# A decode step on one core: eight of its 131 loads get a second DMA with eight outer groups

## The chip, the cores and the metric

One NeuronCore of a Trainium2 chip runs the whole program. The time is device microseconds (us) of one execution. Beside the times of plain runs there is one profiled execution with its trace: instructions of each engine (PE is the matrix engine TensorE with its weight loads PEld, DVE is VectorE, ACT ScalarE, POOL GpSimd, SP SyncE, which here only issues DMAs), the packets of the DMA queues, and the increments of semaphores. The core has 16 DMA engines.

## What is computed

One token goes through a pre-norm attention block with a cache and then a small dense block:

```python
q = (layernorm(x) @ wq).reshape(1, 1, 32, 128).transpose(0, 2, 1, 3)
scores = einsum("bhqd,bhkd->bhqk", q, k_cache) * 128 ** -0.5   # 32 heads, 32768 keys
p = softmax(scores)
o = einsum("bhqk,bhkd->bhqd", p, v_cache)
h = x + o.transpose(0, 2, 1, 3).reshape(1, 1, 4096) @ wo
t = einsum("bsd,df->bsf", layernorm(h), w1) + b1               # 512 -> 1376
out = h + einsum("bsf,fd->bsd", t * tanh(softplus(t)), w2)
```

All data is bf16. The two caches are 256 MB each (MB of 2^20 bytes), the weights some 11 MB. Each byte of the caches is read once and used for one query only. The sum over keys doesn't depend on their order, so long as the K row and the V row of a key stand at the same place.

## The kernel before

**Loads and slots.** The caches are read in halves of a head: 16384 rows of 128 numbers, 4 MB, laid on 128 partitions as 128 rows each, 32 KB a partition in one run. The list `order` (lines 186 to 193) has 131 loads: `wq`; K of head 0 in two halves; then, for t from 0 to 30, K half 0 of head t+1, V half 0 of head t, K half 1 of head t+1, V half 1 of head t; then `wo`, `w12` (w1 and w2, three DMAs) and the two halves of V of head 31. So load 3 is K(1,0), 11 is K(3,0), 16 is V(3,0), 126 is V(30,1), 127 is wo, 128 is w12, 129 and 130 are V(31,0) and V(31,1).

The ring in SBUF has `NS = 6` slots of 4 MB; load i goes to slot i % 6. All loads are issued by SP, in this order (lines 231 to 255). Before load i SP waits until PE has used load i-6 up (line 234, `free_name`), and it issues nothing past such a wait. The last load is cut into four pieces of 64, 32, 16 and 16 rows a partition with semaphores of their own (`TAIL`, lines 195 and 248 to 253).

**Readiness.** A DMA adds 16 to the semaphore of its slot, one for each engine's share. A slot's loads share one semaphore, so `ready_wait` (lines 201 to 203) gives PE the count that stands for "this load and all before it in this slot": 16 times the number of DMAs issued to the slot so far, with two more after w12.

**Work on a half of K** (`k_group`, lines 321 to 346): 16 groups of 8 blocks of 128 rows. PE transposes the 8 blocks into PSUM (line 340), DVE copies the 128 x 1024 result to SBUF (line 343), and two groups later PE multiplies each transposed block with q (line 313, `scores`), which gives one column of 128 scores a block. **Work on a half of V** (`pv`, line 365): 128 matmuls that add up the 128 x 1 output, weighted with the probabilities. Between them stands the softmax of a head (lines 377 to 397): maximum over columns (DVE, 378), over partitions (PE 382, DVE 384), broadcast (PE 387, DVE 389), exponential (ACT 390), sum (PE 395, DVE 397).

**Order on PE** (lines 412 to 422): for each t the first K half of head t+1, the first V half of head t, the second K half, the second V half with the steps of the softmax in between. At the end (lines 435 to 475) come the projections with wo of heads 0 to 30 (431), the softmax sum and b1 (395, 439), V of head 31 (365), its projection (431), the second layer norm (280 to 290), w1 (457), the activation (461 to 467), w2 (472) and the sum (475), whose result SP writes out (256).

**Code.** PE's part alone is 25118 matmuls and as many weight loads. [...]

## Time and profile before

| | |
|---|---|
| median of 3 runs | 1329.84 us (1328.77 to 1330.07) |
| profiled execution: its own time | 1330.19 us |
| profiled execution: span, first to last instruction | 1328.4 us |
| PE busy | 1106.9 us (83%), 25118 matmuls |
| PE weight loads busy | 1073.6 us (81%) |
| DVE busy | 721.7 us (54%) |
| ACT, POOL busy | 20.6 and 1.7 us |
| granted TensorE clock, mean | 0.755 |
| DMA | 551.40 MB in 24080 packets, 415 GB/s over the span |
| PE transposes, line 340 | 8192, 755.7 us, 248 ns each |
| DVE copies, line 343 | 1024, 681.7 us, 692 ns each |
| PE scores, line 313 | 8192, 368.0 us, 166 ns each |
| PE with V, line 365 | 8192, 236.7 us, 164 ns each |
| a 4 MB load of K, issue to landing | 39.6 us, median of 64 |
| a 4 MB load of V, issue to landing | 43.5 us, median of 63 |

Busy times of lines overlap, since PE pipelines its matmuls. In a row of the timeline stand the start in us, the time in us, engine, line, operation, result and sources, how many instructions the row merges, and in brackets the idle time of the engine before it with what ended it; "issue" there means that the profile shows nothing that the engine waited for. The packet is a DMA engine's unit: a partition's run of 32 KB is one packet.

### The profile page before, as it was taken

How to read it: one execution, taken by the hardware profiler on the slowest of the kernel's cores; microseconds unless marked ns; L12 is line 12 of the kernel's file. 1: busy time of each engine (PE TensorE's matmuls, PEld its weight loads, DVE VectorE, ACT ScalarE, POOL GpSimd, SP SyncE). 2: the span in 40 equal slices, each digit the busy share in tenths (PEclk: the TensorE clock that was granted, in tenths of full speed). 3: DMA queues.
4: the chain of work that ended last, by engine and by line, in shares of the span. 5: the costliest groups of instructions: out<-in, count | busy, mean ns of one | idle time of the engine just before them, and what ended most of it. 6: DMA issues, size and time to landing. Idle time of an engine off the chain costs nothing.

```text
span 1328.4 us, 51752 instructions
## 1 busy us (share of the span) xinstructions
PE 1106.9 (83%) x25118; PEld 1073.6 (81%) x25118; DVE 721.7 (54%) x1210; ACT 20.6 (2%) x70; POOL 1.7 (0%) x8
## 2 busy tenths in 40 slices
PE   3887888988888988889889888888888988887984
PEld 3887887888887988888878888788887988887884
DVE  2754655655655654646556556556556555645540
ACT  0000000000000000000000000000000000000000
POOL 0000000000000000000000000000000000000000
PEclk9877868777878777667778667777778677768775
DMA  9999999999999999999999999999999999999974
GB/s 389 429 429 426 432 426 425 433 426 428 431 424 432 427 426 432 425 425 434 426 428 429 425 425 422 424 427 417 428 425 428 425 427 425 426 411 431 383 281 195
DMA packets 24080, 551.40 MB, mean 415 GB/s; under 512 B 2528, under 2 KB 6720, under 8 KB 6976
## 3 DMA queue, kind: packets, MB, share of 16 engines
q1 hardware_dynamic: 23664, 548.09, 96.9%
q8 instruction: 196, 3.21, 1.0%
q14 instruction: 12, 0.10, 0.0%
q10 hardware_dynamic: 144, 0.00, 0.0%
q0 software_dynamic: 64, 0.00, 0.0%
HBM read 548.08 MB, written 0.00 MB: 413 GB/s over the span
## 4 chain that ended last, share of the span: by engine, by line
PE 75%; issue 13%; DVE 8%; DMA 4%; SPq 0%; ACT 0%
PE tps L340 43%; PE ops L365 16%; PE sps L313 12%; DVE ering L343 7%; DMA ring<-in_A_v_cache_dram 2%; DMA ring<-in_A_k_cache_dram 2%; PE hlp L387 1%; PE hlp L382 1%; PE hlp L395 1%; PE sps L457 0%; SPq L229 0%; PE sps L472 0%; PE hlp L282 0%; DVE pmax L378 0%; ACT lns L287 0%
## 5 line engine op out<-in xcount | busy, mean ns | idle before, releaser
L343 DVE COPY ering<-tps 128x1024 bf16<-128x1024 bf16 x1024 | 681.7, 692 | 368.9 <-PE tps L340 365.9
L340 PE MATMUL tps<-identb,ring 128*128 128x128 bf16 x8192 | 755.7, 248 | 35.4 <-issue 31.7
L340 PEld LDWEIGHTS tps<-identb,ring 128*128 128x128 bf16 x8192 | 583.2, 112 | 42.6 <-issue 38.7
L313 PE MATMUL sps<-qT,ering 128*128 128x1 bf16 x8192 | 368.0, 166 | 39.9 <-issue 30.3
L313 PEld LDWEIGHTS sps<-qT,ering 128*128 128x128 bf16 x8192 | 340.4, 101 | 46.8 <-issue 33.5
L365 PE MATMUL ops<-pbuf,ring 128*128 128x1 bf16 x8192 | 236.7, 164 | 114.9 <-issue 106.3
L365 PEld LDWEIGHTS ops<-pbuf,ring 128*128 128x128 bf16 x8192 | 224.7, 101 | 131.6 <-issue 122.7
L373 DVE TENSOR_TENSOR oT<-ops,rtotc 128x1 bf16<-128x1 f32 x32 | 5.1, 161 | 93.5 <-PE ops L365 93.5
L384 DVE TENSOR_REDUCE gmax<-hlp 1x1 f32<-1x128 f32 x32 | 8.9, 279 | 77.2 <-PE hlp L382 77.2
L390 ACT ACTIVATE pbuf<-sps,nbias 128x256 bf16<-128x256 f32 x32 | 15.2, 474 | 1256.5 <-DVE nbias L389 1256.5
L378 DVE TENSOR_REDUCE pmax<-sps 128x1 f32<-128x256 f32 x32 | 13.6, 425 | 17.0 <-PE sps L313 17.0
L387 PE MATMUL hlp<-gmax,onesmat 1*128 1x1 f32 x64 | 18.7, 356 | 2.7 <-issue 2.3
L387 PEld LDWEIGHTS hlp<-gmax,onesmat 1*128 1x128 f32 x64 | 15.8, 303 | 3.7 <-issue 2.4
L382 PE MATMUL hlp<-ident,pmax 128*1 128x128 f32 x64 | 16.9, 357 | 1.7 <-issue 1.2
L282 PE MATMUL hlp<-lns,meanmat 128*128 128x2 f32 x4 | 1.2, 364 | 16.4 <-DVE lns L281 16.4
L282 PEld LDWEIGHTS hlp<-lns,meanmat 128*128 128x128 f32 x4 | 1.0, 313 | 16.5 <-DVE lns L281 16.5
L395 PE MATMUL hlp<-esum,onesmat 128*128 128x1 f32 x64 | 14.2, 292 | 0.0
L389 DVE TENSOR_SCALAR nbias<-hlp 128x1 f32<-128x1 f32 x32 | 5.1, 158 | 13.9 <-PE hlp L387 13.9
L395 PEld LDWEIGHTS hlp<-esum,onesmat 128*128 128x128 f32 x64 | 12.2, 239 | 0.0
L397 DVE RECIPROCAL rtotc<-hlp 128x1 f32<-128x1 f32 x32 | 5.2, 162 | 6.3 <-PE hlp L395 6.3
L274 DVE CAST lnx<-xb 128x4 f32<-128x4 bf16 x1 | 0.2, 171 | 13.6 <-DMA xb<-in_A_x_dram 13.6
L431 PE MATMUL yps<-oT,ring 128*128 128x1 bf16 x128 | 4.7, 172 | 1.9 <-issue 1.6
(43 smaller groups left out, 39.4 us busy)
## 6 DMA issues: line engine op xcount, KB each, us to landing
ring<-in_A_k_cache_dram SPq DMA_DIRECT2D x64, 4096.0 KB, 39.6
ring<-in_A_v_cache_dram SPq DMA_DIRECT2D x63, 4096.0 KB, 43.5
ring<-in_A_wq_dram SPq DMA_DIRECT2D x1, 4096.0 KB, 14.2
ring<-in_A_wo_dram SPq DMA_DIRECT2D x1, 4096.0 KB, 43.5
ring<-in_A_v_cache_dram SPq DMA_DIRECT2D x1, 2048.0 KB, 26.0
ring<-in_B_w_dram SPq DMA_DIRECT2D x1, 1376.0 KB, 39.1
ring<-in_B_w_dram SPq DMA_DIRECT2D x1, 1280.0 KB, 9.2
ring<-in_A_v_cache_dram SPq DMA_DIRECT2D x1, 1024.0 KB, 28.9
```

The costliest lines, as they stand in the source:

```text
L313: S.step(PE, lambda r=r: t_.matmul(S_b[h % 2][:, col0 + r:col0 + r + 1], ering[:, bg % NE, r, :], qT[:, h:h + 1], start=True, stop=True), ...
L340: S.step(PE, lambda r=r: t_.matmul(tb[:, r * 128:(r + 1) * 128], kt[:, gi * GT + r, :], identb[:, :], is_transpose=True, start=True, stop= ...
L343: S.step(DVE, lambda: v.tensor_copy(ering[:, bg % NE, :, :].rearrange("p r d -> p (r d)"), tb[:, :]), name=f"ev{bg}", waits=[f"trb{bg}"] + ...
L365: S.step(PE, lambda r=r, col=col: t_.matmul(o_ps[:, h % 2:h % 2 + 1], vt[:, r, :], pbuf[:, h % 2, col:col + 1], start=(col == 0), stop=(co ...
L373: S.step(DVE, lambda: v.tensor_tensor(oT[:, h:h + 1], o_ps[:, h % 2:h % 2 + 1], rtotc[:, h:h + 1], ALU.mult), name=f"oev{h}", waits=[f"pv{ ...
L378: S.step(DVE, lambda: v.tensor_reduce(pmax[:, h:h + 1], S_b[h % 2][:, 0:SCOLS], AXX, ALU.max), name=f"pmax{h}", waits=[f"qkh{h}"])
L382: S.step(PE, lambda: t_.matmul(A_REG, pmax[:, h:h + 1], ident[:, :], start=True, stop=True), name=f"A{h}", waits=[f"pmax{h}", "ident"])
L384: S.step(DVE, lambda: v.tensor_reduce(gmax[0:1, h:h + 1], A_REG, AXX, ALU.max), name=f"gmax{h}", waits=[f"A{h}"])
L387: S.step(PE, lambda: t_.matmul(B_REG, onesm[0:1, :], gmax[0:1, h:h + 1], start=True, stop=True), name=f"B{h}", waits=[f"gmax{h}", "consts0"])
L390: S.step(ACT, lambda: a.activation(pbuf[:, h % 2, :], S_b[h % 2][:, 0:SCOLS], ACTF.Exp, bias=nb[:, h:h + 1], scale=SC, accum_out=esum[:, h ...
L395: S.step(PE, lambda: t_.matmul(C_REG, onesm[:, :], esum[:, h:h + 1], start=True, stop=True), name=f"C{h}", waits=[f"exp{h}"])
L397: S.step(DVE, lambda: v.reciprocal(rtotc[:, h:h + 1], C_REG), name=f"rcp{h}", waits=[f"C{h}"])
```

## The change

In eight loads, K and V half 0 of heads 3, 11, 19 and 27 (places 11, 16, 43, 48, 75, 80, 107 and 112 of the order), the 4 MB come in two DMAs. The first brings 96 rows a partition (3 MB): partition p gets rows 96p to 96p+95 of the half. The second brings the other 32 rows a partition (1 MB) from the last 4096 rows of the half. Its source pattern has an outer dimension of 8, then 16, then a run of 32 rows: block 8b+a of 32 rows goes to partition 16a+b. Its target is 128 partitions with 8 KB each, as it was. So the rows of a half stand in another order than before, the same one for K and for V. `ready_wait` counts the DMAs of the slot from a table of how many each load has, and gives the same counts as before where no shifted load stands in the slot.

```diff
+    SHIFTED = {(h, 0) for h in range(3, H, 8)}
+    MAIN = 96
+    EXTRA = TPS - MAIN
+
+    def shifted(what):
+        return what[0] in ("k", "v") and what[1:] in SHIFTED
+
+    def dmas(what):
+        return 3 if what[0] == "w12" else 2 if shifted(what) else 1
+
     def ready_wait(what):
         i = where[what]
-        return (ready[i % NS], 16 * (i // NS + 1 + (2 if i % NS == where[("w12",)] % NS and i >= where[("w12",)] else 0)))
+        return (ready[i % NS], 16 * sum(dmas(order[n]) for n in range(i % NS, i + 1, NS)))
...
                     assert at == TPS
+                elif shifted(what):
+                    both = cache[0, h, half * 128 * TPS:(half + 1) * 128 * TPS, :]
+                    start(flat[:, 0:MAIN * Dh], both[0:128 * MAIN, :].rearrange("(p r) d -> p (r d)", r=MAIN), ready[slot])
+                    start(flat[:, MAIN * Dh:], both[128 * MAIN:, :].rearrange("(b a r) d -> a b (r d)", a=8, b=16), ready[slot])
                 else:
                     start(flat, rows, ready[slot])
```

## The prediction

> **What bounds the kernel now.** I read the page first (slices, queues), then the waits, SP's own rows, the tail's timeline, and last the 16 completion increments of each load, which the trace keeps one by one.

> The page's slices and queues:

> ```profile
> DMA  9999999999999999999999999999999999999974
> ...
> q1 hardware_dynamic: 23664, 548.09, 96.9%
> q8 instruction: 196, 3.21, 1.0%
> ```

> The DMA engines never rest before the last two slices. Beside the data (q1) a second queue, q8, fetches PE's code: 196 packets of 16 KB.

> The waits, whole span (engine, line, releaser: total us, times, longest):

> ```profile
> PE ops L365 <- issue: 106.3, 59, 3.2
> ...
> PE ops L365 <- DMA ring<-in_A_v_cache_dram: 8.5, 5, 5.6
> ...
> PE tps L340 <- DMA ring<-in_A_k_cache_dram: 3.3, 1, 3.3
> ```

> PE waits for data six times in all: for the first load, and for the last two. In between it is paced by itself (its work, gaps named "issue", VectorE's copies). Per load the trace agrees: between loads 3 and 126 each K or V has landed 2.5 to 14.6 us before PE's first use of it. Four loads take PE (1250.36-53.33)/30 = 39.9 us (first uses of loads 3 and 123) and the DMA engines, as below, 40.0, so both look full, but the margin is the DMA's.

> The increments show what the mean share hides. Time (us) of the 1st, 8th, 9th and 16th of one load's increments, loads of one ring slot (extracted from the trace):

> ```
> load  issue     1st      8th      9th     16th
>   0    0.74    13.25    13.57    13.79    14.94
>  30  272.74   304.53   307.33   312.35   315.54
>  54  509.03   537.55   542.28   553.07   554.76
>  78  751.09   770.69   777.29   792.78   795.56
> 126 1230.49  1246.01  1248.09  1272.99  1275.83
> ```

> The engines are two groups of eight. The eight ahead need (770.69-13.25)/78 = 9.71 us a load, which is eight 32 KB packets of 1.214 us (median of 16384). The eight behind need (795.56-14.94)/78 = 10.008 us: 0.298 more. That is the code: the q8 packets' durations repeat with period eight (1018, 1018, 1073, 1069, 1060, 1100, 1099, 1087 ns), one per engine in turn, one per engine every 53 us or 5.4 loads, 1.6 us lost each. From load 79 on the eight ahead have nothing queued: their part of a load lands some 12 us after its issue. One of them, the 8th, also lags by 5 us in 78 loads.

> The lag is paid at the end. SP's rows, then PE's:

> ```profile
> 1243.36 0.38 SPq L229 DMA_DIRECT2D ring<-in_A_wo_dram  x1
> 1249.95 32.32 SPq L229 DMA_DIRECT2D ring<-in_B_w_dram  x3
> 1282.32 2.52 SPq L229 DMA_DIRECT2D ring<-in_A_v_cache_dram  x5
> ```

> ```profile
> 1297.91 0.60 PE L439 MATMUL sps<-b1f,ident 128*128 128x11 f32 x2 [0.33 <-DVE b1f L438]
> 1304.07 3.57 PE L365 MATMUL ops<-pbuf,ring 128*128 128x1 bf16 x128 [5.56 <-DMA ring<-in_A_v_cache_dram]
> ...
> 1310.51 1.04 PE L365 MATMUL ops<-pbuf,ring 128*128 128x1 bf16 x33 [0.56 <-issue]
> ...
> 1314.75 0.59 PE L365 MATMUL ops<-pbuf,ring 128*128 128x1 bf16 x16 [0.66 <-DMA ring<-in_A_v_cache_dram]
> ```

> SP hangs in w12's issue from 1249.95: the first of the three lasts 31.1 us, to 1281.05, which is 5.2 us after the engines behind are through load 126 and into wo (4096 packets of 1 KB). The last V loads go out at 1282, though their slots were free at 1265.41 and 1270.67 (PE's last use of loads 123 and 124). PE is ready for them at 1298.51, waits to 1304.07, then follows the pieces to 1315.34; 13.0 us of work follow that nothing shortens.

> **The change, part by part.** The profiled execution took 1330.19 us with a span of 1328.4; the median of the runs is 1329.84, so what I work out against 1330.19 lies 0.3 us above it.

> Issues: 8 more of 0.33 us on SP, which waits 872 + 345 us for free slots; nothing. PE, VectorE and ScalarE run the same instructions; the permuted rows are the same in K and V. The wait of a shifted load now counts 32 increments of its slot: queued behind it on PE is the whole stream, and it costs only if the later DMA lands after PE's first use.

> Transfers: the main DMA moves 24 KB per partition, so 8 packets of 3/4 x 1.214 = 0.911 us per engine, 7.28 us for 9.71: every engine saves 2.43. The second moves 128 pieces of 8 KB. I take it that eight outer groups mean eight engines with 16 pieces each; 8 KB packets exist in before (the tail's 32-row piece: median 0.312 us), so 16 x 0.312 = 4.99 us. New is that an engine's pieces lie 64 KB apart in the cache; the nearest scattered row is wo, 1 KB pieces at 46 ns, so 0.368 us for 8 KB: at most 16 x 0.056 x 8 = 7.2 us more on those eight, and 1 us less at the 24 KB rate. I take 0.312, the same size. Eight engines gain 2.57 us of work a load, eight lose 2.43. Over 8 loads: +20.5 and -19.4 us.

> Which eight? No row of before names an engine, and every load there uses all sixteen. That is the unknown, and it has two ends: the group ahead (forecast), or one with an engine from behind in it (rival A).

> [...]

> If the work goes to the group ahead: the group behind is through load 126 at 1275.83 - 19.4 = 1256.4. The group ahead, never short of work now, at 13.57 + 126 x 9.71 + 20.5 = 1257.5, its laggard some 8 us later (5 us in 78 loads), 1265.6. SP comes free 5.2 us after the last of these, at about 1271, and the last V loads go out at once: 11 us earlier. On that laggard wo (11 us, as the group behind takes from 1275.83 to 1286.86), w12 (7.3, to 1294.12), V 31,0 (9.9) and V 31,1 (10.7) follow one another: the last piece lands at 1304.5 for 1314.7 (1311.7 with the dear 8 KB pieces).

> What is late next is PE itself. At 1298.51 it starts the 256 matmuls with V: 3.57 us for the first 128 (as measured), 4.0 for the rest (the 128 in the rows from 1308.97 sum to 0.99+1.04+1.01+0.59+0.59 = 4.2, 31 to 37 ns each), so 1306.1 without gaps: 9.2 us earlier. But code arrives in blocks of 128 matmuls, and the wait that goes covered its fetch: in before one gap (1310.51, 0.56) was left of two. Uncovered gaps in these phases are 1.6 us (1293.88, project) to 2.7 (mid-run, the chain's longest "issue" pieces). Two of 2.7 leave 3.8 us of gain; I take two of 1.5, near the two nearest rows (0.97 at 1287.67, 1.61 at 1293.89): 1309.1, so 6.2 us. The middle gains nothing, since PE doesn't wait there. Forecast: 1330.2 - 6.2 = **1324.0**, own range 1320 to 1327.

> **Rivals.**

> A, slower: the eight engines of the second DMA are the ones that fetch code, or have one of them among them. Then the engine that is last has 20.5 us more. For: nothing in the trace says otherwise, and it takes only one engine. PE's slack (4 to 14 us) is used up after about the fourth shifted load; the queue behind is never empty from load 0 to the last piece, so all of it reaches the end: 1350.7, or 1347 if the slack and a shorter fetch swallow 3 to 4 us. It decides as soon as one engine is in both sets. Against: the amount, 2 x 20 us between the groups, is that of the lag at 0.298 x 131 = 39 us; this speaks for a balance and not for a side.

> B: the second DMA is dealt to all sixteen engines. Then nothing moves between the groups; 8 x 8 x 34 ns (four 8 KB packets cost 1.248 us for 1.214; half of it on a quarter of the bytes) is below 1 us. 1330 to 1331. For: all loads of before complete with all sixteen.

> C: balance comes, but the tail gives back what it gains: code fetch gaps of 2.7 us and more in the last V phases, or PE 4 us slower in the middle (its slack wandered by 12 us there). 1327.5 to 1330.

> **Numbers.** Forecast 0.55, A 0.33, B 0.05, C 0.07. Within 0.2% (2.7 us), about what a measurement of this kernel can tell from no change: B and most of C, 0.10; of C 0.01 is faster, of C 0.01 slower. Faster 0.56, slower 0.34. Both signs hold much, so the range takes in A: 1319 to 1352; the likeliest case alone is 1320 to 1327.

> **What would show it.** Right: the 9th to 16th increments of load 126 near 1256, within 10 us of the first; w12's issue over in some 20 us for 31.1; no DMA wait of PE before line 365's last 256 matmuls, and gaps named "issue" in them. A: 1st to 16th spread wider than 29.8 us at load 126, and PE waiting for K in the middle. B: increments as now, the spread growing through loads 11 and 16; in the forecast it falls there by 5 us each. Wrong on size: the first 128 matmuls start later than 1299, or PE's middle moves by more than 3 us.

## The result, and the profile after

The changed kernel takes 1431.1 us (median of 4 runs, 1429.48 to 1431.78); the kernel before took 1329.34 us beside it (4 runs). The ratio is 1.0763, 95% interval 1.0745 to 1.0782: 101 us slower. Forecast (1324.0), rival A (1350.7) and the range's upper end (1352) are all far off. The profiled execution took 1430.72 us with a span of 1428.9, 100.5 more than before.

The page's slices and queues after:

```profile
PEclk9876767886778576776777676777777767678775
DMA  9999999999999999999999999999999999999945
GB/s 392 429 429 343 411 343 429 429 427 427 428 429 365 379 321 406 425 428 421 424 427 414 315 353 349 415 423 424 426 429 426 352 362 318 369 387 425 368 159 212
...
q1 hardware_dynamic: 24752, 548.09, 95.8%
q8 instruction: 196, 3.21, 0.9%
```

The DMA engines are as full as before, and q1 moves the same bytes, but the rate now has holes. A slice is 35.7 us; slices 4 and 6 (343) hold loads 11 and 16, and the holes at 13 to 15, 23 to 25 and 32 to 35 hold the other three pairs of shifted loads. Full DMA engines at a lower rate are slow, not idle.

The stretch around load 11 shows how slow (start and end, length, then busy us and number of PE, PEld, DVE, ACT and POOL, granted clock, DMA share, GB/s). After:

```profile
104.00:117.00 13.00, 10.42 (x267) 10.05 (x264) 5.91 (x10) 0.00 (x0) 0.00 (x0) 0.74 1.00 425
117.00:128.00 11.00, 6.23 (x140) 6.10 (x141) 5.51 (x9) 0.00 (x0) 0.00 (x0) 0.86 1.03 241
128.00:140.00 12.00, 8.00 (x188) 7.36 (x186) 2.82 (x7) 0.56 (x2) 0.00 (x0) 0.50 0.99 350
```

The same stretch before:

```profile
117.00:128.00 11.00, 9.59 (x251) 8.84 (x248) 7.26 (x12) 0.00 (x0) 0.00 (x0) 0.87 0.99 423
```

While the second DMA runs, 241 GB/s flow instead of 423, with the DMA share still 1. Single packets in the trace say the same: between 119 and 128 us the 8 KB pieces take a median of 593 ns (0.312 us had been put on them), and the 32 KB packets 2278 ns (1215 before). Between 124 and 128 us on the mean 6.7 engines are in an 8 KB piece and 8.8 in a 32 KB packet, so both halves of the sixteen are slow.

I add up what each of the eight shifted loads loses, from the first to the last 8 KB piece: length of the window times (1 - rate / 427).

```
window, us       GB/s  lost us      window, us       GB/s  lost us
 117.4- 132.4     235     6.8        783.6- 823.5     311    10.9
 175.5- 193.5     232     8.2        846.2- 887.5     316    10.7
 448.7- 476.1     289     8.9       1121.8-1171.6     332    11.1
 508.7- 539.4     281    10.5       1184.1-1236.0     326    12.2
sum of the lost us: 79.2
```

The windows grow longer as the engines drift apart: the last 24 increments of a shifted load spread over 15.8 us at load 11 and over 57.1 at load 112. With the prediction's 20.5 us for uneven bytes, which this run doesn't show apart, 79.2 + 20.5 = 99.7 us, for 100.5 measured on the span.

PE feels it. The waits, after (engine, line, releaser: total us, times, longest):

```profile
PE tps L356 <- DMA ring<-in_A_k_cache_dram: 114.4, 40, 10.9
...
PE ops L381 <- issue: 95.0, 52, 3.6
...
PE ops L381 <- DMA ring<-in_A_v_cache_dram: 25.0, 8, 11.1
```

Lines are 16 further down than before, so L356 is 340. The one wait for K of 3.3 us has become 40 of 114.4 us in all: PE now follows the loads. Its own work is as it was (busy 1102.1 us for 1106.9). The tail's rows on SP and PE:

```profile
1346.18 38.31 SPq L241 DMA_DIRECT2D ring<-in_B_w_dram  x3
```

```profile
1405.59 3.57 PE L381 MATMUL ops<-pbuf,ring 128*128 128x1 bf16 x128 [11.14 <-DMA ring<-in_A_v_cache_dram]
```

SP's hang and PE's wait for V 31,0 have grown (32.32 to 38.31 us, 5.56 to 11.14) where the forecast had them shrink. Load 126's increments fit that; relative to its first: thirteen within 3.3 us, then 25.4, 36.4 and 36.5. Three engines are late, two of them by more than the 29.8 us of before.

### The profile page after: what moved, and what is told of

It reads as the page before. It is cut to its first block, busy times and chain, and to the rows that moved or that the text cites. A ratio compares the mean times of both kernels' runs of the same rounds, so it can differ in the third digit from the quotient of the medians.

```text
span 1428.9 us, 51760 instructions
## 1 busy us (share of the span) xinstructions
PE 1102.1 (77%) x25118; PEld 1069.3 (75%) x25118; DVE 720.7 (50%) x1210; ACT 20.6 (1%) x70; POOL 1.7 (0%) x8
## 3 DMA queue, kind: packets, MB, share of 16 engines
q1 hardware_dynamic: 24752, 548.09, 95.8%
q8 instruction: 196, 3.21, 0.9%
## 4 chain that ended last, share of the span: by engine, by line
DMA 43%; PE 40%; issue 6%; another core or an unknown queue 5%; DVE 4%; SPq 0%; ACT 0%
DMA ring<-in_A_k_cache_dram 41%; PE tps L356 25%; PE sps L329 7%; PE ops L381 6%; DVE ering L359 4%; DMA ring<-in_A_v_cache_dram 2%; PE hlp L403 1%; PE hlp L398 1%; PE hlp L411 0%; SPq L241 0%; PE sps L473 0%; PE sps L488 0%; PE hlp L298 0%; DVE pmax L394 0%
## 5 line engine op out<-in xcount | busy, mean ns | idle before, releaser
L356 PE MATMUL tps<-identb,ring 128*128 128x128 bf16 x8192 | 749.7, 248 | 142.1 <-DMA ring<-in_A_k_cache_dram 114.4
L356 PEld LDWEIGHTS tps<-identb,ring 128*128 128x128 bf16 x8192 | 579.5, 112 | 150.3 <-DMA ring<-in_A_k_cache_dram 118.0
L403 PEld LDWEIGHTS hlp<-gmax,onesmat 1*128 1x128 f32 x64 | 15.9, 305 | 3.3 <-issue 2.2
(43 smaller groups left out, 39.3 us busy)
```

Source lines behind the costliest of these rows:

```text
L356: S.step(PE, lambda r=r: t_.matmul(tb[:, r * 128:(r + 1) * 128], kt[:, gi * GT + r, :], identb[:, :], is_transpose=True, start=True, stop= ...
L403: S.step(PE, lambda: t_.matmul(B_REG, onesm[0:1, :], gmax[0:1, h:h + 1], start=True, stop=True), name=f"B{h}", waits=[f"gmax{h}", "consts0"])
```

## The experiments

The expectations name their theories by letters of their own. E, N and D say that eight outer groups cost something as such (e1, e2, e5 and e6); Q that the split of a load in two does (e1); S that the pieces' source is read slowly (e2 to e4); P, O and W that it costs to write partitions that other engines write too (e2 to e9; no trace names the partitions of an engine, so what O says of them is a supposition, and e5 to e7 test what follows from it); U that partitions 64 to 127 alone are slow for these engines (e7); R that the way there is slow even with nothing else in flight (e9); G that a collision slows all sixteen engines, and L that it slows only those that meet (e10). "Quick" below is an 8 KB packet under 350 ns; medians and counts are of the shifted loads' pieces, without the tail's. Diffs of the first seven and the last are against the changed kernel's second `start` (line 269), of which the first two show the source pattern alone; e4, e5 and e6 also set the number of DMAs in `dmas`. Those of e8 and e9 are against the kernel before, where `extra(i)` is true for the loads named, and `ready_wait` counts three DMAs for them.

**e1: the second DMA in plain order, so on sixteen engines** (a shifted load leaves 32 increments).

```diff
-  both[128 * MAIN:, :].rearrange("(b a r) d -> a b (r d)", a=8, b=16)
+  both[128 * MAIN:, :].rearrange("(p r) d -> p (r d)", p=128)
```

> The second DMA of the eight loads takes its 32 rows a partition in plain order (partition p gets the next 32 rows), so its outer dimension is 128 and it runs on all sixteen engines. Theory E (the price is the eight outer groups, by whatever mechanism): 1330 to 1332 us, 8 KB packets at 0.31 us, no dip in the slices. Theory Q (the price is the split itself, a load in two DMAs with other packet sizes): about 1431 us, 8 KB packets at 0.58 us as in the changed kernel.

Measured: 1330.38 us, ratio 1.0005 (0.9995 to 1.0014). The median 8 KB packet took 311 ns, nearly all were quick, and nothing was lost in the windows. Two DMAs per load, the wait for 32 increments and the 8 KB size cost nothing, so Q falls; what the change pays for is the second DMA's pattern, its eight groups or the order that comes with them.

**e2: sixteen outer groups of 8 pieces.**

```diff
+  both[128 * MAIN:, :].rearrange("(b a r) d -> a b (r d)", a=16, b=8)
```

> The same scattered source order as the change, but with sixteen outer groups (a=16, b=8), so that sixteen engines take part and nothing moves between them. Theory N (the price is that only eight engines run it, so it lasts twice as long on them and they fall behind): 1330 to 1335 us and 8 KB packets near 0.31 us. Theory P (engines that take consecutive partitions write to places in SBUF that another engine writes too) and theory S (8 KB reads a power of two apart are slow at the source): 8 KB packets stay near 0.58 us, other engines' 32 KB packets near 2.3 us while it runs, for about half as long as in the changed kernel: 1350 to 1400 us.

Measured: 1392.07 us, ratio 1.0468 (1.0422 to 1.0513); median packet 561 ns, 104 of 1024 quick. Sixteen groups have eight pieces each, and it is still 62 us slower: N falls, too few groups is not the main cost. The profiled execution (1386.07 us) is 55.9 us longer than before's on the span, and its windows lose 47.9 by the sum above. The other 8 may lie in the engine that is last: load 126's increments spread over 37.0 us, 29.8 before. That isn't shown.

**e3: eight groups, but each group's 16 pieces are read in one run** (other rows than the change's, some from beyond the half).

```diff
+  cache[0, h, 128 * MAIN:128 * MAIN + 8 * 544, :].rearrange("(a x) d -> a x d", a=8)[:, 0:512, :]
+        .rearrange("a (b r) d -> a b (r d)", b=16)
```

> Eight outer groups as in the change, but each engine's sixteen 8 KB pieces lie one after the other in the cache (one run of 128 KB an engine, the runs 136 KB apart). It reads other rows than the reference's for the last quarter of the eight half heads, so keys are left out and others counted twice; the bytes moved are the same. Theory S (the scattered source is slow): 8 KB packets near 0.31 us, no halving, 1330 to 1352 us (what the uneven bytes alone cost). Theory P (the place in SBUF): as the changed kernel, about 1431 us, 8 KB packets near 0.58 us.

Measured: 1427.08 us, ratio 1.0734 (1.0713 to 1.0755), median packet 593 ns. The pieces' distance in the source accounts for some 4 of the 101 us, and the interval overlaps the change's (1.0745 to 1.0782). S falls.

**e4: four DMAs of 32 partitions, eight groups of four partitions each.**

```diff
+  for q in range(4):
+      start(flat[32 * q:32 * (q + 1), MAIN * Dh:], both[128 * MAIN + 1024 * q:128 * MAIN + 1024 * (q + 1), :]
+            .rearrange("(b a r) d -> a b (r d)", a=8, b=4), ready[slot])
```

> The second DMA in four DMAs of 32 partitions each, each with eight outer groups, so that an engine takes four consecutive partitions at a time and not sixteen; the source stays scattered in 8 KB pieces 64 KB apart. Theory P: eight engines now write to eight different groups of partitions, so the halving goes: 8 KB packets below 0.45 us and 1335 to 1375 us. Theory S: unchanged, about 1431 us, 8 KB packets near 0.58 us.

Measured: 1389.9 us, ratio 1.0445 (1.0427 to 1.0462). The packets have two humps: 520 of 1024 are quick, 325 lie between 600 and 650 ns. So half of the pieces are free of whatever slows the rest. P had less, 1335 to 1375 us, since it took all pieces to be free. The windows lose 39.2 us, and 39.2 + 20.5 = 59.7, for 59.8 between the medians and 61.1 on the span.

**e5 and e6: which half.** Of e4's loop, e5 keeps only quarters 0 and 1 (partitions 0 to 63), e6 only 2 and 3 (64 to 127). In both the rows of the other 64 partitions are not loaded, 4 MB of 512.

```diff
+  for q in (0, 1):      # e6: (2, 3)
```

> As the run with quarters, but only the two DMAs for partitions 0 to 63 are kept; the last 32 rows of partitions 64 to 127 aren't loaded in the eight loads (old data of the slot is used, 4 MB less in all). Theory O (an engine writes at full rate only into the partitions that it has in a plain 128-partition load; the first eight engines have 0 to 63): 8 KB packets at 0.31 us, no dip, 1328 to 1332 us if code-fetching engines are among the first eight, 1322 to 1325 if they are all in the other eight (those lose 8 x 2.43 us of work). Theory D (any DMA with eight outer groups halves the rate): dips, 8 KB packets near 0.59 us, about 1360 us.

> The mirror image: only the two DMAs for partitions 64 to 127 are kept, the last 32 rows of partitions 0 to 63 aren't loaded in the eight loads. Theory O: all its 512 pieces of 8 KB near 0.59 us, all sixteen engines at half rate meanwhile, some 4.9 us lost a load as in the run with quarters: 1360 to 1375 us. Theory D: the same as the run for partitions 0 to 63.

Measured: e5 1329.17 us, ratio 0.9986 (0.9977 to 0.9996), 512 of 512 packets quick. e6 1369.94 us, 1.029 (1.0272 to 1.0308), 61 of 512 quick (median 625 ns), and 32 KB packets of 2281 ns (median, 119 to 128 us) in load 11's window. The window between 117 and 128 us in e5, then in e6:

```profile
117.00:128.00 11.00, 10.02 (x253) 9.74 (x251) 8.97 (x14) 0.00 (x0) 0.00 (x0) 0.95 1.01 431
```

```profile
117.00:128.00 11.00, 6.17 (x165) 5.36 (x162) 3.99 (x8) 0.00 (x0) 0.00 (x0) 0.78 1.03 238
```

Same number of groups, same source pattern, same number of bytes; the target partitions differ (and with them the rows read, which e8 and e9 hold the same), and the rate is 431 or 238. D falls. e6's windows lose some 38 us by the sum above, for 39.3 between the medians (42.7 on the span): with half of the pieces left out there are no uneven bytes to add.

By these two runs the quick half of e4 (520 of 1024) is that of partitions 0 to 63: 512 of 512 are quick in e5, 61 of 512 in e6. Yet half of the change's and of e2's pieces go to 0 to 63 as well, and only 47 and 104 of 1024 were quick. Whether the order in which those partitions are written slows them, or the pieces for 64 to 127 beside them, these counts don't tell. Theory O is one reading; which partitions an engine has in a plain load was not shown.

**e7: e5's first DMA four partitions higher** (one DMA to partitions 4 to 35 in eight groups; the other 96 partitions' rows are not loaded).

```diff
+  start(flat[4:36, MAIN * Dh:], both[128 * MAIN:128 * MAIN + 1024, :].rearrange("(b a r) d -> a b (r d)", a=8, b=4), ready[slot])
```

> [...] Theory O: 256 pieces of 8 KB near 0.59 us, the rate of all engines halved for some 2.5 us a load, which is 2.5 x 8 / 2 = 10 us at most on the path, less what the 6 MB left out give back: 1325 to 1340 us. Theory U (only partitions 64 to 127 are slow for these engines): 8 KB packets at 0.31 us, 1315 to 1330 us. The verdict is in the packets' durations.

Measured: 1342.0 us, ratio 1.0073 (1.005 to 1.0096); 88 of 256 packets quick, 108 above 550 ns; the time lies just above O's 1325 to 1340, which takes all 256 to be slow. Shifted by four partitions, still below 64, the quick pieces of e5 become mixed: U, by which all would be quick, falls. Why a third stay quick isn't settled.

**e8 and e9: extra bytes on top of the kernel before**, which leave every load whole. Twenty loads (7, 13, ... 121) also bring 3 KB a partition to a spare buffer in two DMAs of eight groups; e8 to partitions 0 to 63, e9 to 64 to 127. e9 first runs both kinds alone, one after the other, each waited for.

```diff
+  if extra(i):
+      for q in range(2):
+          start(spare[32 * q:32 * (q + 1), :], cache[0, h, 384 * q:384 * (q + 1), :]
+                .rearrange("(b a r) d -> a b (r d)", a=8, b=4), ready[slot])
```

In e9 the target is `spare[64 + 32 * q:64 + 32 * (q + 1), :]`.

> [...] Rival A's term by itself (uneven bytes with a code-fetching engine among the eight): 1346 to 1352 us and no halving. The forecast's view (the eight are the ones ahead): 1329 to 1333 us.

> [...] Theory W (two engines that write the same group of partitions at once get in each other's way, and all engines behind them): alone, both kinds take 0.12 us a 3 KB packet; beside the loads 0.22 to 0.24 us, the rate of all halved meanwhile; time 17.8 us for uneven bytes, 20 x 196 KB at half rate, so 1.9 us each or 37 us, and some 5 us at the start: 1385 to 1395 us. Theory R (the way from these engines to the other half is slow in itself): 0.22 to 0.24 us alone too; the same time.

Measured, e8: 1348.24 us, ratio 1.0127 (1.011 to 1.0143), 17.6 us more. Its eight engines carry 480 KB each, 15 packets of 32 KB or 18.2 us. All of it reaches the end, and nothing runs slower (median 121 ns a 3 KB packet; windows lose 1.9 us). So bytes added to these eight engines alone are paid in full. Load 48's increments say why, relative to the first (480.23 us):

```
0.0  0.4 | 5.8  5.8  5.8  6.0  6.2  10.0 | 11.4  12.9  13.2  13.6  14.6  14.7 | 19.7  19.9
```

By then code has cost its engines 48 x 0.298 = 14.3 us, and the seven extra shares 6.4. Two engines have neither, six (one a laggard) the shares, six the code, two both: the last two are 28.2 us behind at load 120. So two of the eight fetch code.

Measured, e9: 1393.37 us, ratio 1.0477 (1.0459 to 1.0494), 63.2 us more. Alone, the pieces for 64 to 127 take 121 ns, as those for 0 to 63 do; beside loads 588 of 1280 are above 180 ns. R falls: writing 64 to 127 costs these engines nothing by itself, it takes the loads in flight beside it. The windows lose 33.9 us, the start 7.8 (the first load's packet at 9.59 us for 1.75), e8's uneven bytes 17.6: 59.3 of 63.2.

**e10: how far one slow engine reaches** (only partitions 64 to 94 get a second DMA; the other 97 partitions' rows are not loaded).

```diff
+  start(flat[64:95, MAIN * Dh:], both[128 * MAIN:128 * MAIN + 31 * EXTRA, :].rearrange("(p r) d -> p (r d)", p=31), ready[slot])
```

> The second DMA of each shifted load brings only 31 partitions, 64 to 94, in plain order (8 KB each, blocks of 32 rows one after another); the rows meant for the other 97 partitions are not loaded. With 31 pieces, a prime number, it should run on one engine, whose increments show it: 17 in all of a shifted load beside the one soon after the issue. [...] Its own work grows by 31 x 0.312 - 2.43 = 7.2 us a load at the quick rate and by 31 x 0.59 - 2.43 = 15.9 us at the rate of the colliding pieces. Theory G (two writers on a partition slow down all sixteen engines together): while it runs, the 32 KB packets of all engines take near 2.2 us instead of 1.21, the rate falls to some 240 GB/s as in the run with partitions 64 to 127, and its window is some 18 us. Theory L (only the two engines that meet are slowed down, and the sixteen halve in the other runs because eight engines meet eight): 13 or more of the 16 engines keep 1.21 us a 32 KB packet, and the rate stays above 380 GB/s. If the DMA is dealt to sixteen engines after all, or the partitions do not meet, 8 KB packets take 0.31 us and nothing is told apart.

Measured: 1415.77 us (2 runs), ratio 1.064 (1.059 to 1.0691). The 31 pieces run on one engine, one after another in 17.7 us, and the shifted load leaves 18 increments. Their durations repeat with period four, medians 623, 419, 694 and 668 ns in load 11, which would fit an engine for every four partitions, though no trace names one. In load 11's window 145 of 156 whole 32 KB packets stay under 1.5 us (median 1.32), and 11 take over 1.6, up to 2.34. The window:

```profile
117.00:128.00 11.00, 7.94 (x197) 7.19 (x193) 5.30 (x9) 0.00 (x0) 0.00 (x0) 0.70 1.02 383
```

One engine at a time leaves 383 GB/s, e6's eight groups left 238. With one engine G falls and L fits, though the bystanders' 1.32 us lie 9% above its 1.21. That one engine is late by 8 x (17.7 - 2.43) = 122 us, from 13.57 + 126 x 9.71 = 1237 if it is of the group ahead, so at 1359 by load 126, 83 us after the 1275.8 of before; the trace has it at 1364.8, the other fifteen at least 30 us ahead, and 85 us were measured.

So the cause, as far as the runs show it: while the loads run, 8 KB pieces of eight-group DMAs into partitions 64 to 127 take about twice their time (median 625 ns in e6, 311 in e1), and the loads' packets slow down with them (2281 ns in e6, 1214 before); into partitions 0 to 63, dealt as in e5 and e8, or with nothing else in flight (e9: 121 ns for 3 KB), they don't. Four partitions higher (e7) 88 of 256 are quick. That two engines then write the same partitions is the author's reading of it and was not shown.

How far this reaches is not what L says. Beside load 75 of the changed kernel, one engine is in its 8 KB pieces from 803 to 809 us and two from 815 to 823, each time with some fourteen others in 32 KB packets:

```profile
803.00:809.00 6.00, 6.00 (x154) 5.96 (x150) 6.00 (x11) 0.00 (x0) 0.00 (x0) 1.00 1.00 375
815.00:823.00 8.00, 1.13 (x19) 1.03 (x19) 0.32 (x2) 0.56 (x2) 0.00 (x0) 0.50 0.98 232
```

With one, 59 of the 61 packets of 32 KB that start there stay under 1.5 us (median 1.31), as in e10. With two, none of 50 does (median 2.21). So two engines are enough to bring all to half speed, and it doesn't take eight that meet eight, as L has it; by the pattern only four of the change's eight groups (4 to 7) write into 64 to 127 at all. Whether the number decides or which two they are isn't told apart here.

No kernel tried beats the one before; e1 equals it. e5 is 0.1% below it with 4 MB not loaded.

## Why the prediction was wrong, point by point

- **What bounds the kernel** held: the DMA engines. With them late, PE has 40 waits for K.
- **"I take 0.312, the same size"** is the step that failed most. The row was the tail's piece in a 128-partition DMA in plain order. The bound above it ("at most 7.2 us more") came from wo's source pattern, and e3 puts the source at some 4 us. The sizes were right: in e1, with a plain target order, 8 KB took 311 ns and 24 KB 913. What differed was the order of the target, for which the prediction had no term: 593 ns a piece, and 2278 instead of 1215 ns on packets of the *kernel's other loads*. Size: 79 us by the windows.
- **"Which eight?"** was rightly called the unknown, and the likelier end was wrong. e8 shows that the eight are not the group ahead: two of them fetch code, and six do not. e5 agrees: fourteen of load 126's increments lie within 4.7 us, two are 24.1 and 25.2 behind. That the amount equalled the lag, given as an argument for balance, told nothing of the side.
- **Rival A** had the right sign, condition and mechanism: one engine in both sets decides. Its term, bytes paid in full, measured 17.6 of 18.2 us in e8. Its 20.5 us for this change were not measured apart; with the windows they close the sum (99.7 of 100.5, and 59.7 of 61.1 in e4). It was short by the slow packets (79 us by the windows). Its two signs came: a spread of 36.5 us at load 126 (over 29.8) and PE waiting for K in the middle.
- **Rival B** fell: a shifted load leaves 25 recorded increments, 16 + 8 + one that comes some 1.1 us after the second DMA's issue, where e1's leaves 32. So "eight outer groups mean eight engines", which the sum took without a row of before that shows it, held. That only eight share the bytes was weighed at 20.5 us; by e2, which has sixteen groups and loses 62, that is not where most of the time went.
- **Rival C** and the tail's working (gaps of code fetch, 9.2 us earlier) were never put to the test, since the balance didn't come.
- **Issues and compute at nothing** held: e1 has the same issues, wait and instructions at 1.0005.

Open: why bystanders are some 9% slower with one engine (e10) and at half speed with two, what e2's last 8 us are, which engine writes which partitions in a plain load, and what the slow writers share.

## What to carry to other kernels

The same bytes to the same partitions cost nothing here in plain order (e1, ratio 1.0005) and 7.6% in eight groups of 16 partitions (the change, 1.0763): keep every load's order of target partitions the same, and check a DMA of another shape by the duration of its packets *and* of its neighbours' in the same window. A price taken from a row holds for that row's source, size, target and order; a bound must vary each of them. Before moving work between engines, find out which are the slow ones: a small extra load on the candidates alone (e8) reads it off the increments.
